# A recurrence and a gated network in one kernel: other places and banks for the first six chunks, other fills, another order

## The chip, the cores and the metric

The kernel runs on one core of one Trainium2 chip. The time is in device microseconds (us) from start to end of one launch. Five engines work at once, each through its own instructions in order: TensorE (PE; its weight loads are shown as PEld), VectorE (DVE), ScalarE (ACT), GpSimd (POOL) and SyncE (SP), which issues the transfers.

## The reference

Four batches, eight heads, 768 tokens, 48 numbers per head. A recurrence gives y, and a network with a mixing over tokens follows.

```python
for t in range(S):                    # state: 48x48 for each batch and head
    cur = (u * k_t)[:, None] * v_t[None, :]
    y_t = r_t @ (state + cur)
    state = w_t[:, None] * state + k_t[:, None] * v_t[None, :]

h = relu(x @ w_in)                    # x: y of the eight heads side by side, 384
u, v = h[:, :512], h[:, 512:]
v_n = (v - mean(v)) / sqrt(var(v) + 1e-6)
v_s = w_spatial @ v_n + b_spatial     # over the 768 tokens
out = (u * v_s) @ w_out
```

## The kernel before

A batch's 768 tokens are six chunks of 128 tokens; four batches make 24 chunks, numbered through. A chunk has two halves of 64 tokens, because the decay products are taken from a half's start. Two heads share one tile: head 2g stands on rows 0 to 47, head 2g+1 on rows 64 to 111, and there are four such pairs. Matmuls of the recurrence are therefore 64 wide and run in quadrants of TensorE.

Each chunk goes through these steps.

- `slot_load` fetches W (decay), kr (k and r, transposed) and v.
- `slot_prep`: products r*k for the bonus of u (L413, first six chunks only), their sums over a head on TensorE, pg (L418); products of neighbouring decays W2p (L441); the two products of kr with W (L445, one for k and one for r); the running products F and E (L448, L453); kr times F and E (L455, L459); v with its halves swapped, vs (L479); and bv, v times the bonus (L490).
- `slot_a`: scores k x r of a half into the bank tile paw (L524), from there masked into AS (L528).
- `slot_kt`: k transposed to pt (L542) and copied (L546).
- `slot_y`: y into the two banks of py: the bonus as a matmul of bv with the identity (L569, first six chunks), and scores times v (L559).
- `slot_d`: the state's products k x v into paw (L615). `slot_s`: VectorE adds them to the decayed state S1 and writes S0 (L630; L628 for the first). `slot_w`: S0 times the decay gives the next S1 (L640 on ScalarE in four pieces, L642 elsewhere).
- `slot_inter`: r times S1, added to py (L559).
- `slot_x`: y is copied from the first bank (L662) and the second is added (L664), transposed to yt (L668), and split into a high part and a rest (L672, L675 to L680).

Then comes the network: `hv_unit` (ph, L685 to L687, then hv with L714 to L757) per chunk, and per batch `g_unit` (pu, pv) and `out_unit` (po). Each of its matmuls is made of three passes, L685 to L687. Weights are prepared in the first 60 us in a sequence of small steps (L329 to L361): VectorE, ScalarE and GpSimd split them into a high part and a rest.

Who does what, and when, stands in the table PLAN: a word for each operation in program order, its letter the engine (T TensorE, V VectorE, A ScalarE, G GpSimd, S SyncE), the rest the planned start in base 36, hundredths of a microsecond. `issue` emits the operations sorted by that start, so the table sets each engine's order; the real times follow from the waits. An operation's `op({...})` lists the engines that may take it with the planner's costs; these are not part of the program that runs.

`fill` (L894) walks along this order and puts dummy matmuls (`warm`, L890 to L892, written into spare columns of py's first bank) into TensorE's planned gaps of more than 0.3 us, as long as the marker `last` (L969, in chunk 5) hasn't come. One dummy is two matmul rows in the trace, here called a pair.

Buffers: ring "w3" has five tiles, for bv, y, t1 and the weight pieces; "gh" and "gl" have five each, for the gated rows; the PSUM ring "pm" has three, for pt, yt, ph, pg. paw is a tile of two PSUM banks: scores in columns 0 to 255, the state's products in 256 to 447.

At the start SP loads W0 and the first row of u (`u_sb`, L924); `spread` (L931) turns the row into columns up_sb, which pg's matmuls need.

Of the kernel before, what the change touches and what calls it, by code (L numbers as in the profile page):

```python
# [8 lines left out]
F32 = mybir.dt.float32  # L9
F32R = mybir.dt.float32r  # L10
# [6 lines left out]
C = 128  # L17
# [19 lines left out]
V5hp S4y9 A5l7 V6jc S1je A2yj V31r V32u V363 A3d0 V5co S2i5 A3ju V3m4 V3q7 V4h2 A53l V5j1 S2qm A3m6 V4gb V4pq
V504 A5k2 V5o3 S4it V4wy V4zd V51f V55w A5mc V5rn T27w T29t T2e2 A2hs A2jk A2mh S5k S7s Sgo Vur Tyf Vlw Vwp
V1ca Vov Vwg V137 V13w Gzk G1f3 A1un A1ty Gfo V1d8 T1ke V1p8 A1fo T12s A1ax T1ov T1vv T1fr V1j8 A1kc V22l T1ym
A20y V23b T26n A28i T2bq A2ct T2j2 T2lj T2o5 A2t0 A2w8 A2wv Smc Sbd S1es V18w T1lv G1dh V1ml V1jy V1fd G1i1  # L40
V1iv V1nj G1o1 V1ya A29k A2a9 V24n T256 V2da A24j T1r9 A1sr T2c7 T2fz T23t V288 A2dv V302 T2ho A2ju V2ll T2ng
A2pa T2qv A2ry T2ts T2vp T2xm A305 A35x A36k A3bf G3xh V3lw G3x1 G3y9 G3z1 G3zt V40i V41z A457 V4cq A41g A43s
V45n A4aq A4e4 G4im S1do S1fw S224 V28y T2rc G22t G2di V2an V25z V27z V2f3 V2jw G2k5 V2o1 A343 A3aq V2x1 T39s
V3cs A388 T31e A32w T2zj T3jt T382 V3c1 A3e5 V3l0 T3l7 A3py V3s9 T3ur A3w1 T3yq A40e T44m T473 T490 A4cp A4fj
A4jd S1pg S210 S2j9 V2vd T3b9 V2uf V30t V37e V2yd V35u V39n V3ac G39w G3ed A3ut A3hs V3n7 T3i1 V3tl A3ng T3h5
A3in T3vf T41u T3ml V3rj G3ss V3ve T438 A46m V484 T4cs A4ft T4k1 A4l4 T4mp T4pa T4r7 A4ud A4w5 A4wt S2g8 S2lb
S3mk V3hf T3nz G3cr V3j3 V3k2 V3em G3l8 V3mu V3oj G3n3 G3u3 A4a1 V41h V3wv T40d V49f V40q T3qz A3sh T4ax T4dh
T3z7 V47c V4bz T4f7 A4h7 V4io T4ly A4n8 T4ot A4pw T4t4 T4v1 T4wy A4zh A51a A51x A54q V585 V55o G57g V58o V597
G59w V5av V5e0 A5hl V5l3 A5ei A5pt V5tc V5bf A5d2 V5fa T5nq S3rn A47o S4aj A4qy S4tt A56b S596 A5r8 T32a T33q
T36m A3by T5fy T5hy T5je T62h T65d T66t V69k V6ce A6ju G6m7 T356 T3e9 T3fp A3l4 T5ku T5ma T5o0 T5pg T5wo T5y4  # L50
V606 V658 A69o V6gp T3rv T3tb T3xa A3zc T63x T689 T69p T6fi T6l9 T6mp V6or V6qe A6s4 G6ui T4gl T4il T4ki A4tb
T5qw T5sc T5ts T5v8 T5zk T610 V63x V66k A68j V6kn T6rx T6td T6z5 T7aw V7cy S7fg T6w9 T6xp T7cc T7ds A7fu S8gi
T760 T780 T79g T7f8 A7ha S7tx T4yv T50b T537 A559 T6gx T6id T6jt T6o5 T6qh T6ut V6zd G73k A78b V7kw T51r T54n
T563 A58o T7go T7l0 T7mg T7pc T7sy T7ud V7wf V7y2 A89o V8ex T58f T59v T5bb A5j0 T85j T88w T8ac T8d8 T8eo T8g4
V8i6 G8k0 A8my V8pf T6b5 T6cl T6e1 A6g3 T7i4 T7jk T7nw T7rh T7vt T7x9 V7ze V84e A863 V87o T8hk T8j0 T8ro T8t4
A8v6 S945 T8bs T8q7 T8uk T8w0 A8y2 S931 T954 T9b5 T9cl T9e1 A9g3 S9hn S38s S3sr S5u3 S43x G47k V4fd V4ef V4k0
G4p2 V4sc V4t1 G4m7 V52r G683 V6b3 V6dq A6l8 A59q A6fn A6kz A6fe A6h5 A6ug T5eh V6xk T57k V59e V577 T70l T5cr
V5gy V5kc V5pf T72b A73r V759 T7qs A7t0 T87j A88m T8kg T8md T8oa A8qt A935 A93s S3lg S45b S6fh S4w1 G4v8 G4sl
V62z V4xo G5pn V5v0 V67v V5wz V6f0 G6x7 G709 V73c G5v9 G6sw A750 V7fx A759 A75m G7hr T735 V7sx A5vv T6pl A6t9
T7zl T74m V79k V7am V7jq T845 A8c0 V8gl T8xg V8yq T943 A95q T97b T998 T9fh A9mo A9qp A9t5 S5lp S5aa S753 S730  # L60
V6rq G7bm V76x V6t0 V733 V76k V77v V7e9 G7tu V7n5 V7pf V7r2 A8os A7bs A7u2 V7so A7sr A7uo A8fk T81b V8lx A7ku
T7yp A807 T8y4 T82s V85p A8i9 V8l6 T8zu A91u V93b T96k A97u V99d T9he T9k6 T9m3 A9om A9qf A9r8 A9x8 G9vd V9y6
G9yw Ga1i Va27 Ga6j Va79 Vahq Aal5 Vape Aaa3 Aaes Vaj0 Aa84 Aagw Gakx S64d S767 S7st S81z G7g5 V7oh V7m7 V7i1
G7k8 V80p V81d G7qz G8gh V88z V8am V8dm A9lz A8o3 A8z4 A8fb A8w7 G9c2 V91q T918 V9dx G8uv T880 A8at T9o0 T92p
V94p G981 V9fq T9r4 V9t4 V9ur Ta43 Va5d Va7g Tan9 Tapq Taro Aau6 Aavz Aawm S7ec S868 S8fd S90j V83g G8mp G8yd
V8by G8e5 V8g8 V8nq V8wh G94j V8qq V8sd V8un Ga4x Va47 V8w9 A92w V98n G92x G9p6 T9si Va2e G9vt T9jb A9kt Taad
T9pq V9ye G9zn Va18 Tabr Aadr Vaf8 Tajh Vakr Vame Tatk Taw6 Tay3 Ab0m Ab8u Ab9h S7pv S91x S8we S9qf V8tp V9gi
V9ks V901 G97h V98a V9hg V9j4 G9m8 G99c G9do V9lq Gag0 Aag7 A9sw V9nd A9qz A9xr Vabn Ta8w Vade Ga2m T9tz A9w1
Tak5 Ta7q Vaax Vacm Talv Aaox Var2 Tavh Vaws Vaye Tb06 Tb2z Tb4x Ab7f Abb5 Abbs Abdu Vbe2 Vbes Vbfc Vbfv Vbge
Vbgx Vbhg Vbj9 Abr6 Vbt1 Abp7 Abtn Vbvi Vbi0 Abjx Vblr S9rj Aa5r Sa8m Aamk Sapf Ab21 Sb4w Abhk T9vf T9wv Ta2n  # L70
# [48 lines left out]
Tqkl Tqrt Tqt9 Aqvb Sqwv Vn8u Tnlb Vp1v  # L119
"""  # L120

GAP, FILL_TO = 0.3, 5

EARLY = 8

W3 = 5

KR, AB = 3, 2

SPLIT, PE_END = 5, 10  # L130

B_PE = 6

Q = 32
T = D - Q

# [71 lines left out]
def dve(n):  # L208
    return 0.157 + n / 960
# [11 lines left out]
def kernel(  # L221
# [60 lines left out]
    for t in PY:  # L282
        nc.vector.memset(t, 0.0)  # L283
# [761 lines left out]
```

## Time and profile before

| | us |
|---|---|
| median of three runs | 367.86 (366.58 to 367.9) |
| the profiled execution | 367.12 |
| its span, first to last instruction | 365.4 |
| busy: TensorE / its weight loads | 357.3 (98%) / 330.3 (90%) |
| busy: VectorE / ScalarE / GpSimd | 276.4 (76%) / 212.0 (58%) / 136.9 (37%) |

The busy time of TensorE contains the dummies (L892, 19.6 us for 126 rows). The granted clock of TensorE is 1.000 over the span. A line of a view names the line of the kernel, the engine, the operation, and the tile written and those read.

### The profile page before, as it was taken

To read this page: it belongs to the slowest core of one execution; us is meant where nothing else is said; L and a number is where in the kernel's file an instruction comes from. 1 tells how busy PE (TensorE), PEld (TensorE's weight loads), DVE (VectorE), ACT (ScalarE), POOL (GpSimd) and SP (SyncE) were. 2 spreads that over 40 slices of the span, in tenths; PEclk is the share of its full clock that TensorE was granted. 3 is DMA by queue.
4 is the path that set the end of the run, shared out by engine and by line. 5 is a ranking of instruction groups with operands and counts; after the bars stand their busy time and mean duration, and the time that the engine had idled before them with its cause. 6 is when DMAs were issued, how large, how long until landed. Compare 5 with 4: busy or idle time off the path is not lost.

```text
span 365.4 us, 11424 instructions
## 1 busy us (share of the span) xinstructions
PE 357.3 (98%) x4692; PEld 330.3 (90%) x4692; DVE 276.4 (76%) x591; ACT 212.0 (58%) x585; POOL 136.9 (37%) x182
## 2 busy tenths in 40 slices
PE   7999998999999999999999999999999999999998
PEld 7887786799999889899999999899999898899997
DVE  7988996888888978977999865878986877234330
ACT  2467896995455658792554588762454757721212
POOL 3344334412552555533651758133223504013220
PEclk9999999999999999999999999999999999999999
DMA  7995727575155366742446444613462441000101
GB/s 212 266 301 152 220 60 204 156 213 169 45 168 159 104 174 183 213 118 64 117 144 192 129 126 145 197 45 111 117 184 72 119 146 46 2 22 0 36 32 71
DMA packets 21547, 47.82 MB, mean 131 GB/s; under 512 B 2545, under 2 KB 10354, under 8 KB 21490
## 3 DMA queue, kind: packets, MB, share of 16 engines
q1 hardware_dynamic: 21346, 46.85, 43.8%
q8 instruction: 38, 0.62, 0.8%
q14 instruction: 19, 0.16, 0.2%
q10 hardware_dynamic: 144, 0.20, 0.1%
HBM read 42.32 MB, written 4.72 MB: 129 GB/s over the span
## 4 chain that ended last, share of the span: by engine, by line
PE 82%; DVE 7%; ACT 6%; issue 2%; POOL 1%; DMA 1%; DVEq 0%; ACTq 0%; POOLq 0%
PE pv L685 9%; PE pv L687 8%; PE pv L686 8%; PE py L559 6%; PE py L892 5%; PE po L685 5%; PE po L687 4%; PE po L686 4%; PE ph L685 4%; PE ph L687 4%; PE ph L686 4%; PE pu L685 3%; PE pu L687 3%; PE pu L686 3%; PE paw L524 3%
## 5 line engine op out<-in xcount | busy, mean ns | idle before, releaser
L685 PE MATMUL pv<-ws,vh 128*128 128x384 f32 x192 | 65.7, 342 | 0.2 <-ACT us L782 0.2
L687 PE MATMUL pv<-ws,vl 128*128 128x384 f32 x192 | 64.3, 335 | 0.0
L686 PE MATMUL pv<-ws,vh 128*128 128x384 f32 x192 | 64.3, 335 | 0.0
L791 DVE TENSOR_TENSOR t<-pv,b_sb 128x384 f32<-128x384 f32 x32 | 17.6, 552 | 26.5 <-PE pv L687 26.4
L795 ACT CAST gh<-t 128x384 fp32r<-128x384 f32 x32 | 16.0, 514 | 36.7 <-DVE t L793 25.4
L685 PEld LDWEIGHTS pv<-ws,vh 128*128 128x128 f32 x192 | 36.0, 188 | 1.2 <-ACT us L782 0.8
L686 PEld LDWEIGHTS pv<-ws,vh 128*128 128x128 f32 x192 | 36.1, 188 | 0.0
L687 PEld LDWEIGHTS pv<-ws,vl 128*128 128x128 f32 x192 | 36.0, 188 | 0.0
L685 PE MATMUL pu<-xT,wi 128*128 128x384 f32 x96 | 34.2, 357 | 0.0
L685 PE MATMUL po<-wo,gh 128*128 128x384 f32 x96 | 32.8, 342 | 0.0
L687 PE MATMUL pu<-xT,wi 128*128 128x384 f32 x96 | 32.4, 338 | 0.2 <-DVE wi L361 0.2
L687 PE MATMUL po<-wo,gl 128*128 128x384 f32 x96 | 32.3, 336 | 0.0
L686 PE MATMUL pu<-xT,wi 128*128 128x384 f32 x96 | 32.3, 336 | 0.0
L686 PE MATMUL po<-wo,gh 128*128 128x384 f32 x96 | 32.3, 336 | 0.0
L685 PE MATMUL ph<-wi,xT 128*128 128x512 f32 x72 | 30.5, 424 | 1.0 <-DVE bv L490 0.7
L687 PE MATMUL ph<-wi,xT 128*128 128x512 f32 x72 | 28.5, 395 | 0.2 <-DVE xT L680 0.2
L686 PE MATMUL ph<-wi,xT 128*128 128x512 f32 x72 | 28.2, 392 | 0.0
L504 ACT ACTIVATE AS<-id,dgs 128x64 f32<-128x64 f32 x76 | 20.1, 339 | 5.7 <-DVE dgs L496 5.6
L892 PE MATMUL py<-zk 128*128 128x128 f32 x126 | 19.6, 308 | 3.5 <-DVE py L283 2.3
L459 POOL TENSOR_TENSOR kr<-kr,E 112x512 f32<-112x512 f32 x13 | 16.6, 1280 | 14.7 <-DVE kr L445 6.4
L640 ACT ACTIVATE S<-S,prod 112x48 f32<-112x48 f32 x76 | 19.2, 326 | 4.7 <-DVE S L630 3.3
L455 POOL TENSOR_TENSOR kr<-kr,F 112x496 f32<-112x496 f32 x13 | 15.5, 1189 | 16.9 <-DVE kr L445 8.4
(199 smaller groups left out, 958.9 us busy)
## 6 DMA issues: line engine op xcount, KB each, us to landing
kr<-in_tr_dram SPq DMA_DIRECT2D x24, 448.0 KB, 5.0
N<-in_nat_dram SPq DMA_DIRECT2D x18, 384.0 KB, 3.2
Nw<-in_gt_dram SPq DMA_DIRECT2D x16, 384.0 KB, 3.5
W<-in_tr_dram SPq DMA_DIRECT2D x24, 225.8 KB, 3.1
v<-in_nat_dram SPq DMA_DIRECT2D x24, 192.0 KB, 4.1
out_dram<-ot SPq DMA_DIRECT2D x18, 192.0 KB, 3.4
wst<-in_w_spT_dram SPq DMA_DIRECT2D x12, 192.0 KB, 3.8
out_dram<-ot SPq DMA_DIRECT2D x10, 96.0 KB, 3.8
```

What stands on the lines that cost most here:

```text
L455: op({"V": 0.68, "G": 1.07}, lambda e: e.tensor_tensor(seg(kr()[:, 0])[:, :, :L2 - 1], seg(kr()[:, 0])[:, :, :L2 - 1], F()[:, :, 1:].unsqu ...
L459: op({"V": 0.69, "G": 1.1}, lambda e: e.tensor_tensor(seg(kr()[:, 1]), seg(kr()[:, 1]), E().unsqueeze(3).broadcast_to([R, SUB * G, L2, 2]) ...
L504: e.mul(As()[:, j, g, :], id64, dgs()[:, j, g:g + 1])
L524: nc.tensor.matmul(pa()[ks, j, g * L:(g + 1) * L], kr()[rs, 0, ts_], kr()[rs, 1, ts_], start=True, stop=True)
L559: nc.tensor.matmul(py()[row][L * a:L * (a + 1), D * n:D * (n + 1)], x, z, start=(a, row) not in started, stop=not left[0], skip_group_chec ...
L640: e.mul(S1[i % 2][a][:, g, :], S0[:, g, :], Wc[:, g:g + 1])
L685: nc.tensor.matmul(ps, ah, bh, start=first, stop=False)
L686: nc.tensor.matmul(ps, ah, bl, start=False, stop=False)
L687: nc.tensor.matmul(ps, al, bh, start=False, stop=last)
L791: op({"V": dve(HT)}, lambda: nc.vector.tensor_tensor(t1(), pv()[:, :HT], b_sb[:, tsl], ALU.add), r=[(pv, 0), ("b", 0)], w=[(t1, 0)])
L795: op({"A": act(HT)}, lambda: nc.scalar.copy(gh(), t1()), r=[(t1, 0)], w=[(gh, 0)])
L892: nc.tensor.matmul(pw, zk, zk, start=False, stop=True, skip_group_check=True)
```

## The change

1. In chunks 0 to 2 (`PE_SUM`) VectorE no longer adds S1 to the state's products: TensorE adds it in PSUM, by a matmul of the identity with S1 into the same columns of paw (five of them; of six additions the first had nothing to add, but was a copy). The multiply by the decay then reads PSUM (`mul2`: four on ScalarE, two on VectorE).
2. In chunks 0 to 5 (`B_PE`) the scores of head j stand on rows j and go to a tile of the ring "pm" instead of paw. The bonus sums pg are 16 small matmuls into spare columns of paw (`PG`) instead of four whole ones. y of heads j stands in bank j, so one operation (`both`) reads both banks: a copy by ScalarE in chunks 0 to 2 (bv still added by TensorE, now in two matmuls), an addition of bv by VectorE in chunks 3 to 5 (no matmul for bv). The swapped copy vs takes the other head per half.
3. The two products of kr with W are one operation (`pairs`), in all 24 chunks; in the new table 17 stand on VectorE and 7 on GpSimd.
4. bv is in ring "gh" instead of "w3".
5. `fill` places nothing between an operation that y waits for and 0.25 us behind it (`held`), and counts 0.43 us for a dummy up to 7 us and 0.224 later. By the table it now gives 17 + 1 + 1 + 1 + 2 + 2 dummies; before there were 51 in all, with 11 ahead of `spread`. The 17 stand behind `spread`.
6. The first row of u is issued by ScalarE's queue in the setup instead of SP. The two zeroings of py are one.
7. A new table; in the first six chunks two L455, two L459 and two L361 go from GpSimd to VectorE and two L413 the other way. The planner's cost constants change, some of them for parts that stay.

```diff
-            pg = q["pg"] = buf(psM, [P, 512], "pm", f"pg{i}", 3)
+            pg = q["pg"] = buf(psA, [P, 2, 512], "pg", f"pg{i}", 1)
+            pg.make = lambda: paw
...
                 for g in range(G):
-                    nc.tensor.matmul(pg()[:, 2 * g:2 * g + 2], rk()[:, g * C:(g + 1) * C], up_sb[:, g, :],
-                                     start=True, stop=True)
+                    for a in range(SUB):
+                        for j in range(2):
+                            rs = slice(64 * j, 64 * j + D)
+                            ts_ = slice(g * C + a * L, g * C + (a + 1) * L)
+                            nc.tensor.matmul(pg()[L * a:L * (a + 1), j, PG + g:PG + g + 1], rk()[rs, ts_],
+                                             up_sb[rs, g, j:j + 1], start=True, stop=True)
...
-            bv = q["bv"] = buf(pm, [P, DM], "w3", f"bv{i}", W3)
+            bv = q["bv"] = buf(pm, [P, HT], "gh", f"bv{i}", 5, F32R)
...
+        if i < B_PE:
+            pa = buf(psM, [P, 512], "pm", f"sn{i}", 3)
+        else:
+            pa = buf(psA, [P, 2, 512], "sc", f"sc{i}", 1)
...
-                        ks = slice(L * (a ^ j), L * (a ^ j) + L)
+                        row = a ^ j if i >= B_PE else j
+                        ks = slice(L * row, L * row + L)
...
+        if i < PE_SUM:
+            if not first:
+                op({"T": 0.35}, lambda: nc.tensor.matmul(
+                    pa()[:R, a, G * L:G * L + G * D], ident[:R, :R], S1[i % 2][a].rearrange("p g d -> p (g d)"),
+                    start=False, stop=True, skip_group_check=True),
+                   r=[("S1", i % 2, a)], w=[(pa, 0), ("sadd", i)])
+            return
...
+        if i < PE_V:
+            o = op({"A": act(DM, True), "V": dve(DM)}, lambda e: (e.copy if e is nc.scalar else e.tensor_copy)(
+                both(y()), both(pyw)), r=[(py, 0)], w=[(y, 0)])
+        elif i < B_PE:
+            o = op({"V": 0.56}, lambda: nc.vector.tensor_tensor(both(y()), both(st[i]["bv"]().bitcast(F32)), both(pyw), ALU.add),
+                   r=[(py, 0), (st[i]["bv"], 0)], w=[(y, 0)])
...
-        t = first = 1.1
+        t = free = 1.1
         for o in order:
+            if o in held and o.on != "T":
+                free = o.start + o.eng[o.on] + 0.25
             if o.on == "T":
-                if t < last.start and o.start - t > GAP:
-
-                    warm((o.start - t - 0.1) / (0.214 if t > first else 0.43))
+                b = max(t, free)
+                if t < last.start and o.start - b > GAP:
+                    cold = max(0.0, min(o.start, COLD) - b)
+                    warm(max(0.0, cold - 0.1) / 0.43 + max(0.0, o.start - max(b, COLD) - 0.1) / 0.224)
...
-    op({"S": 0.45}, lambda: nc.sync.dma_start(u_sb[:1], u_rep[:1]), w=[("u1", 0)], dma=0.01)
+    nc.scalar.dma_start(u_sb[:1], u_rep[:1])
```

## Rows read from the trace of the kernel before

**Rows 1.** Windows: busy us (count) of PE, PEld, DVE, ACT, POOL; PEclk, DMA share, GB/s.

```profile
10.00:20.00 10.00, 9.44 (x165) 8.23 (x165) 9.38 (x20) 5.48 (x14) 4.15 (x4) 1.00 1.01 284
40.00:50.00 10.00, 9.47 (x113) 7.86 (x112) 9.93 (x20) 8.86 (x28) 3.83 (x4) 1.00 0.44 125
70.00:80.00 10.00, 10.00 (x113) 9.10 (x112) 7.89 (x22) 9.55 (x26) 2.54 (x6) 1.00 0.61 185
300.00:310.00 10.00, 10.00 (x165) 9.07 (x163) 7.74 (x16) 6.63 (x14) 4.49 (x4) 1.00 0.23 74
```

**Rows 2.** The page, part 4: the chain that ended last, by engine.

```profile
PE 82%; DVE 7%; ACT 6%; issue 2%; POOL 1%; DMA 1%; DVEq 0%; ACTq 0%; POOLq 0%
```

**Rows 3.** Waits in 0 to 75 us: us in total, times, longest us.

```profile
DVE bv L490 <- POOL ws L331: 3.2, 1, 3.2
...
ACT hv L750 <- DVE st L742: 2.1, 1, 2.1
...
PEld ph L685 <- DVE bv L490: 0.8, 1, 0.8
```

**Rows 4.** TensorE's timeline: start us, us, operation, [idle before <-releaser].

```profile
2.34 5.32 PE L892 MATMUL py<-zk 128*128 128x128 f32 x24 [2.34 <-DVE py L283]
7.59 0.72 PE L931 MATMUL pu__180<-few,u_sb 1*48 1x1 f32 x16
...
9.02 0.95 PE L418 MATMUL pg<-up_sb,rk 112*128 112x2 f32 x8
...
10.36 0.55 PE L542 MATMUL pt<-ident,kr 112*128 112x112 f32 x4
...
11.52 0.69 PE L524 MATMUL paw<-kr 48*64 48x64 f32 x32
...
15.88 0.82 PE L569 MATMUL py<-bv,ident 128*128 128x384 f32 x2
...
18.90 2.62 PE L892 MATMUL py<-zk 128*128 128x128 f32 x20 [0.56 <-ACT y L662]
21.45 0.67 PE L615 MATMUL paw<-v,KT 64*64 64x48 f32 x32
```

**Rows 5.** VectorE's timeline in the first 60 us.

```profile
8.12 1.63 DVE L455 TENSOR_TENSOR kr<-kr,F 112x496 f32<-112x496 f32 x1
...
22.27 0.36 DVE L630 TENSOR_TENSOR S<-paw,S 112x192 f32<-112x192 f32 x1 [1.27 <-PE paw L615]
...
32.42 0.36 DVE L630 TENSOR_TENSOR S<-paw,S 112x192 f32<-112x192 f32 x1 [0.76 <-PE paw L524]
...
52.41 0.86 DVE L356 TENSOR_SCALAR e_('wo', 1)_866<-e_('wo', 1)_866 128x384 int32<-128x384 int32 x1
...
59.70 0.55 DVE L490 TENSOR_TENSOR bv<-v,pg 128x384 f32<-128x384 f32 x1 [3.20 <-POOL ws L331]
```

**Rows 6.** Lines: busy us, mean ns of one, idle before.

```profile
L640 ACT ACTIVATE S<-S,prod 112x48 f32<-112x48 f32 x76 | 19.2, 326 | 4.7 <-DVE S L630 3.3 <-DVE S L628 1.3
...
L445 DVE TENSOR_TENSOR kr<-kr,W 112x256 f32<-112x256 f32 x32 | 14.7, 468 | 2.0 <-DMA kr<-in_tr_dram 1.8
...
L630 DVE TENSOR_TENSOR S<-paw,S 112x192 f32<-112x192 f32 x40 | 13.9, 348 | 3.8 <-PE paw L615 2.3 <-PE paw L524 0.8 <-POOL S L642 0.6
...
L664 DVE TENSOR_TENSOR y<-y,py 128x384 f32<-128x384 f32 x24 | 13.1, 546 | 4.6 <-ACT y L662 4.4
...
L642 DVE TENSOR_TENSOR S<-S,prod 112x192 f32<-112x192 f32 x12 | 5.7, 479 | 0.1
```

**Rows 7.** Line L455 on VectorE: duration ns min/median/max.

```profile
L455 DVE TENSOR_TENSOR kr<-kr,F x11: 650/666/1630, 8.1 to 267.6; 112x496 f32<-112x496 f32 x11
```

**Rows 8.** GpSimd's timeline around 8 us.

```profile
7.96 1.26 POOL L459 TENSOR_TENSOR kr<-kr,E 112x512 f32<-112x512 f32 x1 [1.97 <-DVE kr L445]
```

**Rows 9.** The tile u_sb: its DMA issues and their landing.

```profile
L924 SPq DMA_DIRECT2D u_sb<-in_u_rep_dram x1: 331/331/331, 1.8 to 1.8; - x1
...
DMA to landing us min/median/max: 3.9/3.9/3.9
```

More of the change, by code (lines that the diff above doesn't have):

```diff
@@ L37 @@
[L37 to L46, printed above, removed]
@@ L130 @@
 SPLIT, PE_END = 5, 10
+PE_SUM, PE_V = 3, 3
+PG = 448
 B_PE = 6
@@ L279 @@
     paw = psA.tile([P, 2, 512], F32, name="paw")
-    PY = [psX.tile([P, 512], F32, name=f"py{n}") for n in range(2)]
+    pyw = psX.tile([P, 2, 512], F32, name="pyw")
+    PY = [pyw[:, n] for n in range(2)]
     pw = PY[0][:, DM:]
-    for t in PY:
-        nc.vector.memset(t, 0.0)
+    nc.vector.memset(pyw, 0.0)
     ident = cp.tile([P, P], F32, name="ident")
@@ L374 @@
     st = [dict() for _ in range(NS)]
+    held = set()
     def slot_load(i):
@@ L443, in slot_prep, with pairs @@
            r=[(W, 0)], w=[(W2, 0)], port=True)
-        for n, key in ((0, "k"), (1, "r")):
-            op({"G": 0.9, "V": dve(half)}, lambda e, n=n: e.tensor_tensor(
-                two(kr()[:, n])[:, :, :, n], two(kr()[:, n])[:, :, :, n], w_()[:, :, :, 1 - n], ALU.mult),
-               r=[(W, 0)], w=[(kr, key)], port=True)
+        def pairs():
+            x = kr()[:, 0]
+            return bass.AP(tensor=x.tensor, offset=x.offset, ap=[list(x.ap[0]), [G * C + 1, 2], [C, G], [2, C // 2]])
+        op({"G": 1.5, "V": 0.69}, lambda e: e.tensor_tensor(
+            pairs(), pairs(), w_().rearrange("p g n q -> p q g n")[:, ::-1], ALU.mult),
+           r=[(W, 0)], w=[(kr, "k"), (kr, "r")], port=True)
         op({"V": 0.69}, lambda: nc.vector.tensor_tensor_scan(
@@ L563, in slot_y @@
         q["mm"] = mm
-        if i < B_PE:
+        if i < PE_V:
             bv = q["bv"]
             def bonus():
-                started.update(((0, 0), (1, 0)))
-                nc.tensor.matmul(py()[0][:, :DM], ident, bv(), start=True, stop=False, skip_group_check=True)
-            op({"T": 0.67}, bonus, r=[(bv, 0)], w=[(py, 0)])
-        elif i == B_PE:
-            op({"V": 0.42}, lambda: nc.vector.memset(py()[0][:, :DM], 0.0), w=[(py, 0)])
+                started.update((a, j) for a in range(SUB) for j in range(2))
+                for j in range(2):
+                    nc.tensor.matmul(heads(py(), j), ident, heads([bv().bitcast(F32)] * 2, j), start=True, stop=False,
+                                     skip_group_check=True)
+            op({"T": 0.72}, bonus, r=[(bv, 0)], w=[(py, 0)])
         def intra():
@@ L635, in slot_w, with mul2 @@
         Wc = prod[:, i, a::SUB]
+        n, bank = (i, a - 1) if a else (i - 1, SUB - 1)
+        if n < PE_SUM:
+            pa = st[n]["pd"]
+            def mul2(e):
+                pd = pa()[:R, bank, G * L:G * L + G * D].rearrange("p (g d) -> p g d", g=G)
+                if e is nc.scalar:
+                    for g in range(G):
+                        e.mul(S1[i % 2][a][:, g, :], pd[:, g, :], Wc[:, g:g + 1])
+                else:
+                    e.tensor_tensor(S1[i % 2][a], pd, Wc.unsqueeze(2).broadcast_to([R, G, D]), ALU.mult)
+            op({"V": 0.36, "A": 0.95}, mul2, r=[(pa, 0), ("Wc", i)], w=[("S1", i % 2, a)])
+            return
         def mul(e):
```

227 lines of the change are left out of this document (125 added, 102 removed).

## The prediction

> **What bounds the kernel now.** I read the windows first. From 70 us to 350 us TensorE is busy for 10.00 us of nearly every 10 us window [rows 1]: the first and a late one stand there, 24 of the 28 show the full 10.00, and the other four lack 0.76 us together. The chain of waits says the same: 82% of the span lies on TensorE [rows 2]. Behind 70 us the time is the sum of TensorE's own work, and an edit to VectorE, ScalarE or GpSimd there can win nothing unless it makes TensorE wait. So time won before 70 us reaches the end one for one, and nothing else does.
>
> Before 50 us VectorE (DVE) is the full one: 9.38 of 10 in the window from 10 us and 9.93 in the one from 40 [rows 1]. TensorE seems just as busy there, but that is dummy matmuls, which the kernel puts into its gaps (51 pairs, two rows to a pair). Third come the waits up to 75 us [rows 3]: VectorE stands 3.2 us at L490 (bv) for a weight piece that GpSimd still has to finish, and behind it ScalarE's normalising L750 waits 2.1 us for VectorE, and TensorE's ph 0.8 us.
>
> The orders of TensorE and VectorE, side by side, show two smaller losses. Ten pairs of dummies run from 18.90, themselves 0.56 us late behind ScalarE's copy of y, and the state products L615 stand behind them until 21.45 [rows 4]; VectorE has nothing else and idles 1.27 us before its L630 at 22.27. At 32.42 it idles 0.76 us more for paw, in which the scores L524 still are [rows 5].
>
> **The change, part by part.** The sum is made against the profiled execution of 367.12 us (span 365.4); the median of the runs shown is 367.86, so I add 0.74 at the end.
>
> *Fills.* 51 pairs become 24; none is placed between a chunk's y matmuls and the read of y any more, so pd no longer stands behind them. I count both idles before L630, 1.27 + 0.76 = 2.0 us [rows 5]: **-2.0**, ends -2.0 and 0 (if the S0 chain is late for another reason).
>
> *Another ring for bv.* bv leaves w3 for gh, so L490 doesn't wait for a weight piece. VectorE idles 3.20 us [rows 5], ScalarE 2.1 behind it, TensorE 0.8 [rows 3]. Those are the ends, -0.7 and -3.2. Bv is read by TensorE late, so not all of VectorE's idle passes; I take ScalarE's **-2.1**, the wait nearest the middle, because hv follows it.
>
> *VectorE's work in the first six chunks.* Off: six state sums at 0.348 = 2.09, three y adds at 0.546 = 1.64, and 11 products L445 at 0.468 = 5.15 [rows 6] against six joint ones; a joint one has 512 elements, so I price it like L455 with its 496, 0.67 [rows 7]: 4.0. On: two state multiplies, 0.479 as in L642, = 0.96 [rows 6]. The new table also takes two L455, two L459 and two L361 back from GpSimd, 6 x 0.67 = 4.0 by the median of L455 on VectorE [rows 7], and gives two L413 away, of the same size, -1.3; single output and weight pieces that change sides come to about +0.5. Together -2.09 - 1.64 - 1.15 + 0.96 + 4.0 - 1.3 + 0.5: **-0.7**. Ends -3.9 (of the additions only the multiplies count) and 0.
>
> *Fewer collisions of VectorE and GpSimd.* L455 took 1.63 us at 8.12 [rows 5], where its median is 0.666 [rows 7], while GpSimd ran L459 from 7.96 for 1.26 us [rows 8]. Seven VectorE operations up to 53 us are drawn out like this beside a GpSimd operation; the first and the last stand in [rows 5], and with their own medians taken off they lose 4.3 us in all. Thirteen GpSimd operations of 0.9 us or more stand there; the new table has eight. I take 5/13 of 4.3: **-1.65**, ends 0 and -4.3. The Trainium skill has a rule for this, "SBUF — State Buffer", section "Who interferes with whom": a VectorE instruction with two SBUF inputs contends with a GpSimd instruction that reads SBUF, and the second to issue is blocked until the first has finished. By that rule L455 would lose the rest of L459, 7.96 + 1.26 - 8.12 = 1.10 us; the trace has 0.96, so it agrees. By it an operation that reads PSUM doesn't collide, and that would leave the y reads and the PSUM multiplies free of it.
>
> *TensorE's own work before 70 us.* Bonus products: 8 matmul rows, 0.95, become 16 of a quarter of the tile; the scores' 32 such ones take 0.69, so 16 take 0.35: 6 x -0.6 = -3.6. The bonus matmul on bv goes in three chunks, -0.82 each = -2.4, and is split in the others, +0.3. Five state sums are new; half the columns of bv's matmul, 0.41 each: +2.0. Scores now use two of the four quadrants instead of all four; if a pair then no longer overlaps the next, they take up to twice the 0.69; the middle is +0.35: +2.1 [rows 4]. That is -1.6, from -3.7 (scores as now) to +0.4 (twice). TensorE isn't the bound here, since it has room for dummies, so only little passes: **-0.2**, with the same ends.
>
> *The first dummies.* Before, 12 pairs ran from 2.34 in 5.32 us, 0.44 each, and the spread of u, waiting for its row, came at 7.59; its row was issued at 1.83 and needed 3.9 us [rows 4, 9]. Later ten pairs take 2.62 us, 0.26 each. Now ScalarE issues the row once it is free, about 2.6, so it lands at about 6.5; then the spread; then 17 pairs stand between it and the first pt, which ran at 10.36 [rows 4]. If the pace rises at 7.4, where it rose before, the block ends at about 6.5 + 2 x 0.44 + 15 x 0.26 = 11.3. If the row is late (block from 7.2) and as many pairs as before, 12, run at the early pace, it ends at 7.2 + 12 x 0.44 + 5 x 0.26 = 13.8. If the row lands sooner it ends by 10.4. I take **+1.2**, ends 0 and +3.4: the first case, which keeps the time of the rise that the rows show, and a little for a later landing.
>
> *Costed at nothing.* The joint product in chunks 6 to 23, the merged memset and the reordered swaps: TensorE's 10.00 of 10 covers them [rows 1]; if that cover were gone, 18 x 0.2 us of VectorE would show. The other cost constants change no instruction. State sums read PSUM from ScalarE: four pieces of 0.326 as today [rows 6].
>
> Moving pg into paw lets the scores leave it: the 0.8 us wait at L630 goes. In return bv's read of pg must be over before the state products enter paw. "PSUM — Partial Sum Buffer", section "PSUM bank collisions raise a hardware error", of the Trainium skill asks that accesses be ordered by bank and quadrant and not by address. By that rule six reads of bv hold the products back, up to one bv of 0.54 each, 3.3 in all; no row here shows such a wait. I leave it outside the sum.
>
> Sum: -2.0 - 2.1 - 0.7 - 1.65 - 0.2 + 1.2 = -5.45. 367.12 - 5.45 = 361.67, plus 0.74: **362.4 us**.
>
> **The rivals.**
> 1. *The opening starts late.* The block of 17 pairs holds pt, and with it the state products and the scores of chunk 0, by the full 3.4 us: 362.4 - 1.2 + 3.4 = 364.6. For it: the pace was 0.44 for all 12 first pairs [rows 4], and now nothing runs on TensorE ahead of the spread but one pair. Against it: VectorE's L455, which pt needs, ended at 9.75 [rows 5] anyway.
> 2. *More comes free.* All of the 4.3 us of collisions, 3.2 of the ring, and no late opening: 362.4 - 2.65 - 1.1 - 1.2 = 357.5. For it: VectorE is full, so any shortened row counts. Against: five GpSimd operations less can't free seven places.
> 3. *Hidden anyway.* TensorE in 10 to 50 us is near 9.4 to 9.9 of 10 [rows 1]; if it is its real work and the landing of loads that set the opening, the removed waits are filled by others and none of the sum's 5.45 arrives: 362.4 + 5.45 = 367.9, no change.
> 4. *Slower: the state sums stand in TensorE's queue.* Before, VectorE added S1 while TensorE went on. Now each of the five sums waits in order for ScalarE's multiply (four pieces of 0.326, about 1.0 with the overlap of starts [rows 6]), takes 0.35 to 0.41, and adds about 0.3 of handing over, 1.67 in all, with pt, scores and y of the next chunk queued behind it. Fully exposed that is 8.3 us: 362.4 + 8.3 = 370.7. It decides from 1.1 us exposed per sum, where the 5.45 is spent. For it: TensorE runs in order, and the dummies show that whatever stands ahead of pd is paid. Against it: the same chain existed with a VectorE hop in it.
>
> **How the numbers follow.** Forecast 0.46 (its own range 360.0 to 365.0), rival 1 0.18, rival 2 0.12, rival 3 0.14, rival 4 0.10. The range that holds 8 in 10 takes the forecast and rival 1 whole, and a little over half each of rivals 2 and 3, down from and up to their own times: 357.0 to 368.2. What a measurement of this kernel can tell from no change is 0.5%, 1.84 us; so faster means below 366.0. The forecast and rivals 1 and 2 lie there: 0.76. Rival 3 is the same, 0.14; rival 4 is slower, 0.10.
>
> **What would show it.** In the profile after: no idle of VectorE before the state multiply that ends at TensorE's fills; bv without GpSimd ahead of it around 55 to 60 us and hv without the 2.1; fewer VectorE rows over 0.9 us; pt of chunk 0 at about 11.5. TensorE's first full window comes some 5 us sooner. The forecast falls if the sums wait over a microsecond each on ScalarE, if pt(0) comes at 13 or later and the delay stays, or if the windows behind 70 us are no longer full.

## The result: 0.7% slower, and the profile after

The changed kernel takes 369.96 us (median of five, 368.84 to 370.91), the kernel before 367.67 beside it: ratio 1.0067, 95% interval 1.0046 to 1.0087. The forecast was 362.4 us, faster than before. The profiled execution took 369.96 us, its span is 368.3.

I follow the forecast with one measure, TensorE's lead: the matmul records of both traces are added up in order, dummies left out, and the times at which the same share of that work is done are compared (minus: the changed kernel is ahead). It is worked out from the traces. From 70 us on a few tenths are uncertain (half a microsecond at 300); at 35 and 60 us, where the two tables put single pieces in another order, the number depends on how the records are weighted by some microseconds, and no reading below rests on these two:

| share done by before at, us | 35 | 60 | 70 | 90 | 130 | 200 | 250 | 300 | 360 |
|---|---|---|---|---|---|---|---|---|---|
| changed kernel | -3.3 | -4.5 | -5.1 | -4.6 | -3.8 | -2.0 | +1.2 | +2.7 | +2.6 |

At 70 us the lead is 5.1, almost the sum of 5.45; then 7.7 us are given back. Three windows before, and then the windows after (columns as in [rows 1]), show where:

```profile
100.00:130.00 30.00, 29.61 (x502) 27.81 (x503) 26.66 (x55) 17.23 (x53) 15.03 (x19) 1.00 0.52 146
...
220.00:250.00 30.00, 29.96 (x282) 28.09 (x282) 21.18 (x49) 20.04 (x51) 13.60 (x17) 1.00 0.37 115
...
280.00:300.00 20.00, 19.82 (x322) 17.96 (x314) 16.59 (x35) 13.13 (x38) 6.57 (x9) 1.00 0.40 117
```

```profile
10.00:20.00 10.00, 8.34 (x207) 7.59 (x207) 7.07 (x13) 4.32 (x14) 2.42 (x3) 0.98 0.78 225
...
40.00:50.00 10.00, 10.00 (x161) 9.04 (x160) 9.43 (x24) 8.94 (x24) 3.07 (x6) 1.00 0.50 163
70.00:80.00 10.00, 9.95 (x117) 9.33 (x116) 9.71 (x23) 9.94 (x25) 1.91 (x3) 1.00 0.58 180
...
100.00:130.00 30.00, 29.00 (x497) 26.55 (x496) 28.79 (x57) 14.19 (x48) 15.59 (x16) 1.00 0.56 163
...
220.00:250.00 30.00, 28.78 (x346) 26.26 (x345) 21.46 (x44) 18.93 (x47) 11.44 (x19) 1.00 0.44 132
280.00:300.00 20.00, 18.88 (x335) 16.77 (x334) 17.12 (x35) 12.04 (x37) 10.03 (x11) 1.00 0.29 84
```

Behind 70 us TensorE is no longer full: 1.00 us is missing in 100 to 130, 1.22 in 220 to 250, 1.12 in 280 to 300, where before 0.39, 0.04 and 0.18 were missing. Added up over the matmul records behind 70 us, TensorE idles 4.9 us (before 0.8): 3.0 of them it waits for VectorE, 0.4 for ScalarE, in 1.1 nothing that the trace shows holds it, and the rest is in small pieces. The idles are 4.1 of the 7.7. The other 3.6 lie in longer records of the same matmuls: behind 95 us those of the recurrence take some 1.8 us more and the output products 0.8. What lengthens them is not shown.

The chain of waits, part 4 of the page, has moved with it; TensorE had 82% and VectorE 7% in [rows 2]:

```profile
PE 65%; DVE 21%; issue 5%; ACT 5%; POOL 2%; DMA 1%; POOLq 0%; DVEq 0%
```

A piece of that chain in order of time (start us, us, what), behind 280 us:

```profile
282.06 0.48 PE pyw L586 x24
...
283.72 0.73 DVE AS L552
284.45 0.23 DVE S L659
284.69 0.46 DVE y L727
285.15 0.47 DVE dg L484
...
285.65 0.32 DVE dgs L510
...
285.98 0.95 DVE dgs L510
286.93 0.26 DVE S L659
287.19 0.47 DVE xT L737
...
287.68 0.57 DVE xT L745
...
288.38 0.47 PE ph L750
```

From 283.7 to 288.3 the chain runs through VectorE's queue alone: the mask (AS), y, the diagonal steps (dg, dgs), two state sums (S) and both parts of xT, for which the next ph waits. TensorE runs dry for 1.0 us ahead of this ph. ScalarE stands idle for 2.8 us of this stretch, behind the load of v. The new table moved work to VectorE behind the first six chunks too. The output copies (line, duration, first and last start) show it, first before and then after:

```profile
L811 ACT COPY ot<-po x21: 459/480/484, 105.2 to 361.6; 128x384 f32<-128x384 f32 x21
...
L811 DVE COPY ot<-po x3: 557/558/559, 104.2 to 345.4; 128x384 f32<-128x384 f32 x3
```

```profile
L876 DVE COPY ot<-po x12: 531/556/558, 95.7 to 363.1; 128x384 f32<-128x384 f32 x12
L876 ACT COPY ot<-po x12: 471/480/481, 99.9 to 364.1; 128x384 f32<-128x384 f32 x12
```

Before, 3 stood on VectorE and 21 on ScalarE; after, 12 and 12. In all, VectorE is busy for 282.2 us after against 276.4 before, ScalarE for 199.7 against 212.0.

### The profile page after: what moved, and what is told of

Read it like the earlier page. It is cut to its first block, busy times and chain, and to the rows that moved or that the text cites. A ratio compares the mean times of both kernels' runs of the same rounds, so it can differ in the third digit from the quotient of the medians.

```text
span 368.3 us, 11532 instructions
## 1 busy us (share of the span) xinstructions
PE 355.6 (97%) x4792; PEld 328.0 (89%) x4792; DVE 282.2 (77%) x589; ACT 199.7 (54%) x535; POOL 133.9 (36%) x172
## 4 chain that ended last, share of the span: by engine, by line
PE 65%; DVE 21%; issue 5%; ACT 5%; POOL 2%; DMA 1%; POOLq 0%; DVEq 0%
PE pv L750 6%; PE pv L751 6%; PE pv L752 6%; PE pyw L586 5%; PE pu L750 4%; PE pu L752 4%; PE pu L751 4%; PE pyw L957 3%; PE ph L750 3%; PE po L750 3%; PE ph L752 3%; PE ph L751 3%; PE po L752 2%; PE po L751 2%; PE paw L643 2%
## 5 line engine op out<-in xcount | busy, mean ns | idle before, releaser
L858 POOL TENSOR_TENSOR t<-t,us 128x384 f32<-128x384 f32 x13 | 13.6, 1047 | 43.0 <-DVE t L856 25.1
L779 ACT ACTIVATE hv<-ph 128x512 f32<-128x512 f32 x24 | 14.2, 592 | 17.0 <-PE ph L752 17.0
L847 ACT ACTIVATE us<-pu 128x384 f32<-128x384 f32 x32 | 15.4, 485 | 9.1 <-PE pu L752 9.1
L750 PEld LDWEIGHTS pu<-xT,wi 128*128 128x128 f32 x96 | 18.0, 188 | 2.6 <-DVE KT L570 0.9
L861 POOL TENSOR_TENSOR gl<-t,gh 128x384 fp32r<-128x384 f32 x13 | 15.1, 1163 | 11.8 <-ACT gh L860 11.8
```

The costliest lines, as they stand in the source:

```text
L750: nc.tensor.matmul(ps, ah, bh, start=first, stop=False)
L779: op({"A": 0.61}, lambda: nc.scalar.activation(hv(), ph(), AF.Relu, accum_out=col(0)), r=[(ph, 0)], w=[(hv, 0), (s, 0, j)])
L847: op({"A": act(HT, True)}, lambda: nc.scalar.activation(us(), pu()[:, :HT], AF.Relu), r=[(pu, 0)], w=[(us, 0)])
L858: op({"V": dve(HT), "G": pool(HT)}, lambda e: e.tensor_tensor(t1(), t1(), us(), ALU.mult), r=[(us, 0)], w=[(t1, 0)], port=True)
L861: op({"G": pool(HT), "V": dve(HT)}, lambda e: e.tensor_tensor(gl(), t1(), gh().bitcast(F32), ALU.subtract), r=[(t1, 0), (gh, 0)], w=[(gl, ...
```

## The experiments

Below, "seam at T" means: the changed table up to T, behind it the words (order and engines) of the kernel before, moved forward; code is that of the change except where shown. The kernel before took 367.3 to 367.5 us beside them. The leads at 70, 90, 130 us and at the end:

| kernel | 70 | 90 | 130 | end | median us | ratio to before [95%] |
|---|---|---|---|---|---|---|
| e1 seam at 83 | -4.4 | -3.9 | -1.1 | -1.3 | 367.35 | 1.0005 [0.9985, 1.0025] |
| e2 the same, joint product kept | +0.9 | +1.4 | +4.9 | +4.5 | 368.43 | 1.0008 [0.998, 1.0036] |
| e3 opening of before, rest of the change | -0.1 | -0.2 | -0.1 | +6.2 | 374.28 | 1.0186 [1.013, 1.0242] |
| e4 change, 11 output copies back | -4.0 | -3.4 | -3.0 | -0.4 | 367.57 | 1.0012 [0.9992, 1.0032] |
| e5 change, bv first | -4.7 | -4.2 | -3.3 | +1.6 | 369.17 | 1.0041 [1.0019, 1.0064] |
| e6 change, 8 more pairs | -6.1 | -5.6 | -5.1 | +1.0 | 368.25 | 1.0014 [0.9991, 1.0037] |
| e7 e1, bv first | -3.1 | -2.6 | +0.2 | +0.3 | 366.09 | 0.9948 [0.9923, 0.9973] |
| e8 e7, 8 more pairs | -4.6 | -4.1 | -1.2 | -1.5 | 366.12 | 0.9958 [0.9927, 0.999] |
| e9 e7, 16 more pairs | -1.0 | -0.5 | +2.4 | +2.7 | 368.24 | 1.0019 [0.9997, 1.0041] |
| e10 change, engines of before behind 83 | -3.1 | -2.5 | -0.2 | +7.7 | 375.82 | 1.024 [1.0212, 1.0268] |
| e11 change, bv in ring w3 | -0.7 | -0.1 | +0.8 | +4.5 | 369.18 | 1.0062 [1.0027, 1.0098] |
| e12 e7, whole pg matmuls | -3.2 | -2.7 | +0.1 | -0.2 | 366.89 | 0.9983 [0.9965, 1.0] |
| e13 seam at 105 | -4.9 | -4.4 | -3.0 | -3.3 | 365.27 | 0.9955 [0.9932, 0.9978] |
| e14 e13, bv first | -7.0 | -6.5 | -5.2 | -5.0 | **363.26** | 0.9898 [0.9875, 0.9921] |

The lead is that of one profiled execution. The profiled ones of e1, e13 and e14 were the fastest of their kernel, 1.0 to 1.4 us under the median; those of e7 and e9 lie 1.6 us above it, those of e2 and e11 3.1. In the traces of e2, e7, e9, e10 and e11 the stop and the lower clock described in the last section fell between 58 and 68 us. Against the 3.5 us that the changed kernel gains between 56 and 69 us they took 2.5 to 4.5; for these kernels compare the change of the lead, not its level. Even kernels with the same opening differ by 1.1 us at 70 us (change, e1, e4, e13).

**Which part loses it: e1 to e4.** e1's seam joins 83 us to 88.25, moved by 5.25 (its expectation says 88.5 and 5.5).

```diff
+SPLIT_KR = range(8, 24)
...
+        if i in SPLIT_KR:
+            for n, key in ((0, "k"), (1, "r")):
```

> The changed kernel up to 83 us of its table, and from there the order and the engines of the kernel before (its table from 88.5 us on, moved 5.5 us forward; the two kr x w products apart again in chunks 8 to 23). Theory A (the opening's gain of 4.6 us is real and is given back only because the new table loads VectorE more behind 83 us): 367.7 - 4.6 = 363.1, range 362 to 364, TensorE's windows behind 90 us full again. Theory B (the joint product, not the order, costs the time behind 83 us): the same 363, so this run alone does not tell them apart. Theory C (work done earlier in the opening is owed later: loads, weight pieces and the rings hold TensorE whatever the order): 366 to 370.

> As the run before, but with the joint kr x w product in all chunks. Theory A: within 0.7 us of that run, about 363.1: a joint product takes 0.68 us on VectorE and 1.53 on GpSimd against two of 0.42 and two of 0.87. Theory B: the joint product costs most of the 7.1 us lost behind 90 us, so 5 us or more above the run before, 368 or later. Theory C: like the run before, 366 to 370.

> The reverse: the kernel before up to 88.5 us of its table, and from there the order and the engines of the new table, moved 5.5 us back, with the joint product in chunks 8 to 23. Theory A: 367.7 + 7.1 = 374.8, range 372.5 to 376. Theory B: about the same. Theory C: 367 to 369, since nothing was done early that would be owed.

e4 changes 11 words of the table, the output copies, in this way (five of the words, without what stands between them):

```diff
-V6nq V93b V8vq Vdcz Vd9a
+A6nq A93b A8vq Adcz Ad9a
```

> The changed kernel with one thing different: eleven copies of the output rows behind 83 us, which the new table took from ScalarE to VectorE, stand on ScalarE again, at the same places of the order. That takes 11 x 0.55 = 6.1 us off VectorE. Theory A in its strong form (VectorE's sum of work is the bound there): 370.0 - 3 to 5 = 365 to 367. Theory A in its weak form (the order of the operations, not VectorE's sum): 368.5 to 370.5. Theories B and C: 370.0, no change.

e3 is clear: with before's opening, which holds the lead at zero up to 130 us, the new order and its joint products lose 6.2 us by the lead and 1.9% by the ratio. Its windows show the same empty places as the changed kernel's:

```profile
130.00:160.00 30.00, 28.87 (x485) 24.52 (x484) 24.89 (x53) 22.16 (x59) 14.09 (x19) 1.00 0.55 162
...
280.00:300.00 20.00, 18.97 (x336) 16.90 (x335) 17.10 (x32) 10.56 (x34) 9.18 (x10) 1.00 0.35 101
```

e1 was not: the lead lost 2.8 us between 90 and 100 us in one step and was flat behind it. That left open whether the opening leaves a debt on VectorE, or the stitch itself costs this. e2's lead is flat behind its step as well, so the joint product in the later chunks is worth little: the ratios of e1 and e2 are alike (1.0005 and 1.0008). So the loss of e3 belongs to the order and the engines. e4 falls between the theories: by the medians the copies are some 2.4 us of the loss, and by the lead what is given back between 70 us and the end falls from 7.7 to 3.6.

**The wait of bv: e5, e7.** In the first 75 us VectorE has a new wait (waited for, us, times, longest):

```profile
DVE bv L504 <- ACT S L681: 3.7, 2, 2.9
...
DVE bv L504 <- PE paw L663: 1.7, 1, 1.7
```

bv reads pg, which now lies in paw. The new table emits the state's products, the state sum (L663) and ScalarE's state multiply (L681) of the same tile ahead of it, so bv waits for them:

```profile
13.95 0.55 DVE L504 TENSOR_TENSOR bv<-v,paw 128x384 f32<-128x384 f32 x1 [2.87 <-ACT S L681]
...
23.86 0.56 DVE L504 TENSOR_TENSOR bv<-v,paw 128x384 f32<-128x384 f32 x1 [1.68 <-PE paw L663]
...
28.68 0.56 DVE L504 TENSOR_TENSOR bv<-v,paw 128x384 f32<-128x384 f32 x1 [0.81 <-ACT S L681]
```

Five words put bv of chunks 0 to 2 first (the words alone, without what stands between them):

```diff
-Tt2 Trp Ato V1ev V1pp
+Trp Tuc Aue V1bd V1pc
```

> The changed kernel with five starts of its table moved: bv of chunks 0 to 2 reads its bonus sums out of paw before the state products (or the state multiply) of the same tile are put into the order, so that VectorE's L504 has no state multiply of ScalarE to wait for. In the changed kernel's trace VectorE idles 5.4 us before L504. Theory D (this idle is what kept VectorE from gaining in the opening): the idle is gone, TensorE's lead over the kernel before at 35 us grows from 3.2 to 5 us or more, and the time falls by 1 to 3 us to 367 to 369; not by all 5.4, since the later order still loads VectorE. Rival E (VectorE would have stood there anyway, for TensorE's or ScalarE's next piece): lead at 35 us unchanged within 0.7, time 370.0.

> The first run's kernel (new opening, order of the kernel before behind 83 us: 367.4) with the five moved starts of bv, products and multiply. Theory D together with A: VectorE arrives at the seam earlier, TensorE no longer waits for it at 91 to 98 us (2.75 us lost there), time 367.4 - 2 to 3.5 = 364 to 365.4. Rival E: 367.4 within 0.7.

The wait does not go, it shrinks: to 3.2 us in e5, 2.0 in e7 and 1.9 in e14, from 5.4 in the changed kernel and 6.4 in e13. These are e14's lines:

```profile
DVE bv L517 <- ACT S L694: 1.1, 1, 1.1
DVE bv L517 <- ACT y L732: 0.8, 1, 0.8
```

In the changed kernel it brings 0.8 us, inside the spread, and e5's lead at 70 us is not larger than the changed kernel's; e5's time, 369.2, lies between theory D's range and rival E's 370.0, and the lead at 35 us, by which its expectation wanted to judge, is too uncertain. Ahead of the later order of before it brings 1.3 us (e7 against e1; 366.1 is above the 364 to 365.4 that theories D and A gave together), and in the pair e14 against e13 2.0 us by the medians, with intervals apart. Of these 2.0 some 0.5 are the clock (below): between the runs with the same mean granted clock, 0.995, the difference is 1.5 us (six of e13 with a median of 364.7, four of e14 with 363.3). e7 is already faster than both kernels.

**Dummies and the clock: e6, e8, e9.** 

```diff
+                if o.start in (11.46, 14.03, 15.9, 18.96):
+                    warm(2)
```

> The changed kernel with eight more pairs of dummies: two pairs each ahead of four TensorE steps planned between 11 and 19 us. In the changed kernel's trace the granted clock is 0.5 between about 19 and 23 us, after TensorE had stood idle for parts of 14 to 19 us; in the kernel before it is 1.00 throughout. Theory F (the dummies taken away kept the clock up): granted clock 1.00 in 18 to 24 us, the scores of chunk 1 take 1.1 instead of 1.86 us, time 370.0 - 1 to 1.5 = 368.5 to 369. Rival (eight pairs of 0.25 cost the 2 us that they take, in TensorE's order): 370 to 371.5, whatever the clock.

> As the run before, with the eight more pairs of dummies too. Theories A, D and F together: 363 to 364.5, granted clock 1.00 up to 100 us, faster than both kernels. If the dummies only cost: 1 to 2 us above the run before. If VectorE is the bound at the seam: like the run before, since TensorE's gain is lost in the wait.

> The kernel with the moved bv and the order of the kernel before behind 83 us (366.1), with sixteen more pairs of dummies at five TensorE steps of the opening, five of them ahead of the bonus sums of chunk 1 and five ahead of the state part of y of chunk 5. At these two places its trace has gaps of 1.3 and 2.5 us within a group of small matmuls that wait for nothing the profile shows, a 16 KB transfer of kind 'instruction' ahead of each, and the granted clock at 0.5 for some microseconds after. Theory G (small matmuls run ahead of TensorE's code, the gap takes the clock down): with the dummies there the gaps shrink or are filled, clock 1.00, and since TensorE has 2.7 us to spare at the seam, the dummies cost nothing: 363.5 to 364.7. Rival (the gaps move with the dummies): clock 0.995 or less and 366 as before, or 367 with the dummies' 4 us.

In e6 the clock held (1.00 in 20 to 22 us, where the changed kernel had 0.50), its lead at 70 us is 1.0 us larger, and its median is 1.7 us below the changed kernel's, with the two ratios' intervals apart. The same pairs on e7 bring nothing in the median (e8), and e9's 16 pairs cost 2.1 us, though nine of its ten runs have a mean clock of 1.000. But in e8's profile the pairs didn't hold the clock: it is 0.50 in 20 to 22 us. In its ten runs the mean granted clock tells the times apart. Four with 1.000 took 363.6 to 365.0 us, three of them inside the 363 to 364.5 that theories A, D and F gave together, and six with less took 365.9 to 368.4. In e13, too, six runs with 0.995 took 364.0 to 365.2 and six with 0.991 took 365.3 to 367.9. In e6, which has the later order of the change, there is no such difference (seven with 1.000, median 368.3; three with 0.995, 368.1). So where the later order is that of before, less of the clock goes with 1 to 3 us more (between the medians of such groups of runs 1.2 us in e7, 1.9 in e13, 2.8 in e8), the stop ahead of it included; in the changed kernel the two cost between nothing and 1.7. They aren't its main loss: e3 loses its 6.2 us with the clock at 1.00 in its trace.

**Engines, ring, pg: e10 to e12.** e10 gives 243 operations behind 83 us back to the engines they had before, in the new order. e11:

```diff
-            bv = q["bv"] = buf(pm, [P, HT], "gh", f"bv{i}", 5, F32R)
+            bv = q["bv"] = buf(pm, [P, DM], "w3", f"bv{i}", W3)
```

e12 makes pg of four whole matmuls again, in paw:

```diff
+                    nc.tensor.matmul(pg()[:, 0, PG + 2 * g:PG + 2 * g + 2], rk()[:, g * C:(g + 1) * C], up_sb[:, g, :],
+                                     start=True, stop=True)
```

> The changed kernel (370.0) with its own order and starts throughout, but behind 83 us each operation on the engine that it had in the kernel before (243 operations change engine); the joint products stay. Strong form of theory A (the new table's choice of engines is the loss behind 90 us): 364 to 366, TensorE's lead at 300 us -2 or more instead of +2.7. Weak form (the order of the operations as much as the engines; an engine choice taken out of its order fits badly): 367.5 to 371.

> The changed kernel (370.0) with bv in ring w3 again instead of gh. The prediction's term: the other ring gives 2.1 us (0.7 to 3.2); so TensorE's lead at 70 us falls from 5.1 to about 3.0, the time is 370 to 372. Rival (the wait at 59.7 us belonged to the old order, in which a weight piece came late on GpSimd, and not to the ring): lead at 70 us within 0.7 of 5.1, no VectorE wait for a weight piece at bv, 370.0.

> The same kernel (366.1) without more dummies, but with the bonus sums pg of chunks 0 to 5 as four whole matmuls per chunk again (8 rows instead of 32 in the trace), both heads' columns in one bank of paw. Theory G: fewer instructions in the group behind y of chunk 0, no gap of 1.0 to 1.8 us in it, clock 1.00 around 19 to 23 us, pg 0.3 us longer each: 364.3 to 365.3. Rival (the gap belongs to a place in the order and not to the number of instructions): a gap of the same length in the next group, clock and time as before, 366 to 366.6.

e10 is the slowest of all: an order fits the engines it was made for, and it can't be said by single moves what the later order costs. It lies above its weak form's 371 too. In e11 bv is back in w3 and doesn't wait for a weight piece; the median is that of the changed kernel within 0.8 us, with runs from 367.4 to 372.7. Up to 56 us, ahead of the stop in its trace, its lead is that of the changed kernel within 0.5. e12 is 0.8 us above e7, intervals overlapping; the stop at pg went, but others came (last section), as the rival had it.

**The stitch or a debt: e13, e14.** Their seam joins 105 us to 109.75, moved by 4.75, where fewer operations are displaced; products split in chunks 10 to 23.

```diff
+SPLIT_KR = range(10, 24)
```

> The changed kernel's own table is kept to 105 us (e1 left it at 83), from there stands the order and the engines of the kernel before, moved 4.75 us forward, with the w products split again in chunks 10 to 23. Theory A (the new table's later order gives the won time back, and the step of 2.75 us that every kernel with a seam at 83 us showed between 90 and 100 us belongs to that seam, where pieces of both orders meet): TensorE's lead of 3.7 to 4.0 us at 105 us is kept to the end but for the 0.3 us by which the later order of before drifted in e1, so 363.7 to 364.5 us against 367.4 beside it. Rival D (the opening of the change leaves VectorE a debt of some 2.75 us, which is paid at whatever place the later order begins): the same step at about 110 us, a lead of 1.0 to 1.3 us at the end, 366.1 to 367.4.

> e13 with the three bv products of each chunk's group ahead of the two state operations that they waited for (as in e7, which ran 1.3 us faster than e1). Theory A with the wait on ring paw as a price of its own: 0 to 1.5 us below e13, 362.8 to 364.3 us. Rival D: the step comes at 110 us whatever the lead, 365.5 to 366.5 us.

The step doesn't come again: between 90 and 130 us e13 and e14 lose 1.4 and 1.3 us, where the changed kernel loses 0.8 and e1 2.8. From 130 us on e13's lead stays at -3.0 to -3.4, and e14's is -5.2 at 130 and -5.0 at the end. So most of the step of 2.8 us was the stitch at 83 us, there is no debt of that size, and what is won up to 130 us reaches the end if the order behind it is the one of before; of e14's 7.0 us at 70 us, 5.0 do. e13's median is 0.8 us above theory A's range and 0.8 under rival D's; its interval reaches rival D's (0.9978 is 366.6 us), and it is the lead, not the time, that speaks against a step. e14's median lies in theory A's range. Its windows are full again where the changed kernel's were not, and behind 70 us TensorE idles 1.0 us in e13 and in e14, instead of 4.9:

```profile
100.00:130.00 30.00, 29.63 (x419) 26.94 (x409) 27.81 (x53) 14.94 (x48) 17.55 (x20) 1.00 0.56 162
...
220.00:250.00 30.00, 30.00 (x285) 28.18 (x284) 23.01 (x56) 17.31 (x46) 10.28 (x12) 1.00 0.38 112
280.00:300.00 20.00, 20.00 (x327) 18.14 (x326) 16.09 (x35) 13.39 (x37) 7.89 (x10) 1.00 0.37 111
```

e14 is the best of all, 4.2 us under before and, by the medians, 6.7 under the changed kernel.

## Why the prediction was wrong

**The step that failed** is the premise "time won before 70 us reaches the end one for one", with "costed at nothing ... TensorE's 10.00 of 10 covers them". I counted the table's moves in the first six chunks only, and took the full windows of [rows 1] as a property of TensorE's work. They were a property of the order behind it. The new table replaces that order in all 24 chunks, and behind 70 us it gave back 7.7 us. That the order does it is shown from both sides: the new order behind the old opening loses 6.2 us (e3), and the old order behind the new opening keeps what it has at 130 us (e13, e14). By which operations is shown in part: 3.0 us of waits for VectorE in the trace, and the output copies that it was given (e4). The prediction's own test, "if the windows behind 70 us are no longer full", is what came. With the later order of before, the forecast of 362.4 is missed by 0.9 us only (e14), though e14 also has bv first; with the change's own opening (e13) by 2.9. Even then the premise holds only from 130 us on.

**Inside the opening** the sum came out, 5.1 for 5.45, but not by its terms; that they add up to it is in good part luck. TensorE's records give an account of their own up to 75 us, by what each adds to its busy time: dummies take 6.5 us less (15.9 before, 9.4 after) and its other new and changed work 1.3 us more. And 3.5 of the 5.1 us arise in one place: taken at the transposes of y, the lead is 1.6 at 56 us and 5.1 at 69.
- *Fills, -2.0.* The two idles of [rows 5] ahead of the state operation are gone. The price of fewer dummies, a lower clock, was not in the sum.
- *Another ring, -2.1.* The waits of [rows 3] are gone, and the 3.5 us between 56 and 69 us lie where they were. But in e11 they stay away with the old ring: they belonged to the old order, not to the ring.
- *Collisions, -1.65.* Instead of seven drawn-out VectorE operations up to 60 us there are two, together 0.6 us over their 0.68, where the seven lost 4.3: so 3.7 of VectorE's time, nearer to rival 2. How much of it reached TensorE is not shown, and the number changes from run to run: with bv first, e14 has no such operation up to 60 us and e5 two that lose 1.3 us.

```profile
17.03 0.97 DVE L469 TENSOR_TENSOR kr<-kr,F 112x496 f32<-112x496 f32 x1
...
30.93 0.98 DVE L360 SCALAR_TENSOR_TENSOR e_('wv', 1)_515<-d_('wv', 1)_336,e_('wv', 1)_515 128x512 int32<-128x512 int32 x1
```

- *pg into paw, left outside the sum.* VectorE waits 5.4 us for it, more than the 3.3 I named, and about as much as the idles removed from [rows 5] (1.27 + 0.76 + 3.20 = 5.2). It held bv back, not the state's products as I had it, since the table puts bv last. The shorter wait is worth 1.5 to 2.0 us at the end (e13, e14). The rule that the prediction names from "PSUM — Partial Sum Buffer", section "PSUM bank collisions raise a hardware error", of the Trainium skill fits where the kernel waits: the operations ahead of bv touch the same tile at other columns. The wait is the program's own ordering; no run here shows what would happen without it.
- *TensorE's own work, -0.2.* It was to fall by 1.6 us and rose by 1.3, outside its ends. The scores of six chunks take 6.8 us instead of 3.5 (1.1 a chunk instead of 0.69 [rows 4], and 1.86 at the lower clock). The bonus sums fell from 5.5 to 3.2 and not by 3.6: I took 16 matmuls for 16 rows, but the trace has 32 rows a chunk, 0.61 to 0.64 us. The bonus matmuls fell by 2.0, the state sums added 2.2. And that TensorE has room for dummies holds only up to 31 us, where the last dummy ahead of 70 us stands: the 9.47 of 10 in the window from 40 us [rows 1] are its real work.
- *VectorE's work, -0.7.* No run singles it out.
- *The first dummies, +1.2.* The spread ran at 3.6, not 7.59: the row landed sooner, and pt of chunk 0 came at 10.82 instead of 10.36, so +0.46. The dummies' pace rose at 9.4 us, not at the 7.4 that I kept from before; the block still ended at 11.0, since it began at 4.67. This is the start of TensorE's timeline:

```profile
10.82 0.55 PE L566 MATMUL pt<-ident,kr 112*128 112x112 f32 x4
...
12.79 1.11 PE L548 MATMUL sn<-kr 48*64 48x64 f32 x31
```

**The rivals.** Rival 4 gave 370.7, near the result, but by luck and for a wrong reason: the state sums (L663) take 2.7 us in all, and TensorE waits 0.3 us ahead of them, once. Rival 1 falls with the early row. Rival 3 falls, since e14 shows that the opening's gain is not hidden.

**Open:** which moves of the later order cost the rest beside the output copies, and why the same matmuls' records are longer in it. e10, with all engines put back at once, is slower still, so the engines can't be judged apart from the order. What the seams themselves cost is known only for the one at 83 us.

## What to carry to other kernels

A window at 10.00 of 10 said here that the bound engine was fed by the order that was there, not that any order would feed it: when a table is made anew, compare the load of each engine along the chain behind the bound one, stage by stage, also where the change "does nothing". When a small tile moves into a bank of another step, look who is emitted first: here its reader waited for users of other columns of the tile that stood ahead of it. And before a gain in the opening is called lost, run the new opening with the old rest, with the seam where few operations are displaced.

## What the runs showed of the hardware

TensorE's granted clock is 1.00 throughout in the records before [rows 1]. Even so, the first dummies' rows stand 0.21 us apart up to 7.2 us (9.3 after) and 0.11 behind that, so that the early pace has to be read from the rows. After, the granted clock fell to 0.50 of 2.4 GHz, the level of 1.2 GHz, in 20 to 22 us (windows, columns as above):

```profile
18.00:20.00 2.00, 1.52 (x29) 1.51 (x30) 1.97 (x4) 0.90 (x5) 0.00 (x0) 0.92 0.91 248
20.00:22.00 2.00, 2.00 (x30) 1.78 (x30) 1.20 (x3) 1.95 (x5) 0.00 (x0) 0.50 0.85 234
22.00:24.00 2.00, 2.00 (x50) 1.92 (x47) 0.32 (x2) 0.73 (x2) 1.27 (x1) 0.73 1.02 325
```

Ahead of it TensorE was busy for 1.44, 1.48 and 1.52 of 2 us in the windows from 14 us, partly because of a stop in the middle of a group, for which the trace shows no wait:

```profile
18.48 0.52 PE L428 MATMUL paw<-up_sb,rk 48*64 48x1 f32 x21 [0.99 <-issue]
...
20.62 1.86 PE L548 MATMUL sn<-kr 48*64 48x64 f32 x29
```

29 rows of the scores then took 1.86 us, where 31 took 1.11 at 12.79. Such a stop can be longer. In e7, at 60 us (windows):

```profile
60.00:62.00 2.00, 0.00 (x0) 0.00 (x0) 0.00 (x0) 0.34 (x2) 0.00 (x0) 1.00 1.05 213
62.00:64.00 2.00, 1.88 (x23) 1.63 (x23) 1.26 (x3) 0.83 (x2) 0.00 (x0) 0.70 1.00 244
64.00:66.00 2.00, 2.00 (x7) 1.60 (x7) 2.00 (x4) 0.97 (x4) 1.32 (x1) 0.50 0.74 221
```

TensorE stood 2.52 us, VectorE waited 3.29 us for its y, and the clock fell behind it. e7's lead is 3.1 us at 70 us, where e14, with the same opening, has 7.0. In both traces a 16 KB transfer of the kind "instruction" had started shortly before (15.93 us after, 59.09 in e7). With pg as whole matmuls the stop at pg went and others came at 25.8 and 34.6 us (1.02 and 0.94 us, e12). That the transfers are the cause fits in time, but was not shown by an experiment, and the kernel before has them too (17.80 and 23.24 us) without a stop of this length.
